# Landmarks laid over all 128 partitions, with the order of every engine's work written out

## The chip, the core and the metric

The kernel runs on one core of one Trainium2 chip. The metric is the device time of one execution in microseconds, lower is better, and the number that counts is the median over runs. In this text PE is the matrix engine (PEld its weight loads), ACT, DVE, POOL and SP are the other engines with their own instruction queues, and each of them takes its instructions strictly in the order in which the program has them.

## What is computed

Eight batches of attention through 32 landmark vectors per head, and then a two-layer network on the joined heads:

```python
def sm_attn(qq, kk, vv):
    s = scale * np.matmul(qq, kk.transpose(0, 1, 3, 2))
    a = softmax(s)
    return np.matmul(a, vv)
p_packed = sm_attn(p, k, v)              # p: (8, 8, 32, 64), q, k, v: (8, 8, 576, 64)
out = sm_attn(q, p_packed, p_packed)     # (8, 8, 576, 64)
x = out.transpose(0, 2, 1, 3).reshape(4608, 512)
h = x @ w_in                             # (512, 2048)
g = where(h >= 1, h, where(h <= -1, 0, (h + 1)**2 / 4))
result = g @ w_out                       # (2048, 512)
```

The landmarks are summed over in the second attention, so their order within a head can be any, as long as it is the same everywhere.

## The kernel before

**Tiles.** Everything is multiplied in bf16 with sums in f32. Tokens of a batch lie on 96 partitions. For each batch b (function `attention`, line 454) the keys and queries are transposed (tiles `tp`, `kT`, `qT`; on PE by line 471 for batches 0 and 1, by a transposing DMA of SP on line 500 for the others). Line 528 multiplies keys with landmarks into `sp` (four score tiles of a pair of heads each in batch 0), line 533 takes their exponentials `ex` on ACT, lines 619 and 624 form the packed values `pk`, line 634 the sums of the exponentials, and line 271 (a shared copy helper) casts them into `ppT`. Line 700 multiplies queries with `ppT` into `s`; on ACT follow the exponentials `eT` (line 723), the logarithm `ln` of their sums (line 732, sums `sm` on PE by line 728) and the reciprocal `rc` (line 737); DVE makes `A` from them (line 742). In place of out @ w_in, line 686 multiplies `ppT` with w_in into `mp`, which is cast to `M`: four chunks f of 512 hidden units. The function `hidden` (line 806) then does, for each of the 16 groups fi of 128 hidden units, four matmuls `h<-A,M` on PE (line 814), `x` on ACT (line 820), `t` on DVE (line 828) or on ACT (line 830), and `hT` on DVE (line 835). The function `output` (line 872) does 16 matmuls `o<-w_out_sb,hT` (line 889) for each tile of 128 tokens, a copy `ob` and a store (line 908). There are 36 such tiles, so 576 matmuls of 512 columns (608 instructions, since the last tile is done in three parts).

**Loads.** POOL issues the loads of k, q, v and of the weights (lines 352, 363, 368), which cast f32 to bf16 on the way. Eight of these may be under way; the ninth waits on POOL until the first has landed. The first half of batch 0's keys (`k_raw`) and the landmarks of batches 0 and 1 (`p_raw`) come as f32 over SP and ACT.

**Landmarks.** `p_raw` is a tile of 32 partitions (landmark), two batches, 8 heads by 64: two DMAs of 64 KB, one from SP and one from ACT (line 395). DVE casts it to `p_nat` (line 446); eight transposes of 32 rows on PE (line 426) put the head dimension on partitions (`tpp`), and four copies (line 271) place them into `pT`. The landmarks of batches 2 to 7 (`p_late`) come in six DMAs of POOL (line 375), four batches on 128 partitions and two on 64, with eight transposes (line 421) and four copies.

**What sets the order.** Each piece of work is a `Task` with a rank, the engines on which it can run and the time that each takes; a `Plan` runs through a model of the engines before anything is emitted, and at each step gives an engine that task of lowest rank among those that can start soonest (`run(slack)`). The program is then emitted in that order. The ranks are computed from the numbers `AT`, `HID`, `OUT` and `L1`. Where PE would wait before the first `o` matmul, the end of the kernel function fills the planned gap with matmuls on zeros (`o<-zeros`, line 942). PSUM has three wide buffers (tag `w`, for all of `tp`, `sp`, `pk`, `s`, `sm`, `mp`, `h` and a few `o`) and two narrow ones for `o`.

Of the kernel before, what the change touches and what calls it, by code (L numbers as in the profile page):

```python
# [11 lines left out]
class Task:  # L12
# [4 lines left out]
    def __init__(self, rank, ways, deps=(), takes=(), mode=None, behind=()):  # L17
        self.rank, self.ways, self.deps = rank, ways, list(deps)
        self.behind = [d for d in behind if d is not None]
        self.takes, self.frees, self.mode = list(takes), [], mode  # L20
        self.start = self.end = self.engine = None
        self.users = []


class Plan:
# [8 lines left out]
    CLAIM = 0.3  # L34
# [4 lines left out]
    def __init__(self, buffers):  # L39
# [8 lines left out]
    def add(self, rank, ways, deps=(), takes=(), mode=None, behind=()):  # L48
# [41 lines left out]
    def run(self, slack):  # L90
# [7 lines left out]
        ready = [t for t in self.tasks if not waiting[id(t)]]  # L98
        done = []

        def served(users):
            for u in users:
                waiting[id(u)] -= 1
                if waiting[id(u)] == 0:
                    ready.append(u)

        def finished(t):
# [5 lines left out]
            served(t.users)  # L113

        while len(done) < len(self.tasks):
            best = None
            found = defaultdict(list)
            left = {b: sorted(v) for b, v in self.slots.items()}
            for t in sorted(ready, key=lambda t: t.rank):
                at = max((d.end + self.LATENCY for d in t.deps), default=0.0)  # L120
                at = max([at] + [d.start + 0.001 for d in t.behind])
                need = defaultdict(int)
                for b in t.takes:
                    need[b] += 1
                short = any(len(left[b]) < n for b, n in need.items())
                wants = at < self.free["PE"] + self.CLAIM
                for b, n in need.items():
                    if not short:
                        at = max(at, left[b][n - 1] + self.LATENCY)
                    if wants:  # L130
                        del left[b][:n]
                if short:
                    continue
                for e in t.ways:
                    if e == "SP" and self.held is not None:
                        continue
                    start = max(self.free[e], at)
                    if e == "PE" and self.mode is not None and t.mode != self.mode:
# [839 lines left out]
```

## Time and profile before

| what | value |
|---|---|
| runs | 243.48, 244.42, 244.64 us; median 244.42 us |
| span of the profiled execution, first to last instruction | 241.1 us |
| between that span and the median | 3.3 us |
| PE busy / PEld busy | 97% / 56% of the span |
| ACT / DVE / POOL busy | 80% / 74% / 13% |
| granted PE clock | 1.00 |
| data moved by the DMA engines | 37.03 MB, mean 154 GB/s |

The page gives the profiled execution's span and no other time of it; the runs' times hold 3.3 us more than that span, which is work around the program that the profile doesn't show. A row of a timeline gives the start in us from the start of the span, the length, the engine, the line, the operation with its tiles, and in brackets how long the engine had been idle and what ended that. PE's busy time counts overlapping matmuls, so it says that PE had work in hand, not how fast it went; the distance between the starts of neighbouring matmuls tells that.

### The profile page before, as it was taken

To read this page: it belongs to the slowest core of one execution; us is meant where nothing else is said; L and a number is where in the kernel's file an instruction comes from. 1 tells how busy PE (TensorE), PEld (TensorE's weight loads), DVE (VectorE), ACT (ScalarE), POOL (GpSimd) and SP (SyncE) were. 2 spreads that over 40 slices of the span, in tenths; PEclk is the share of its full clock that TensorE was granted. 3 is DMA by queue.
4 is the path that set the end of the run, shared out by engine and by line. 5 is a ranking of instruction groups with operands and counts; after the bars stand their busy time and mean duration, and the time that the engine had idled before them with its cause. 6 is when DMAs were issued, how large, how long until landed. Compare 5 with 4: busy or idle time off the path is not lost.

```text
span 241.1 us, 5370 instructions
## 1 busy us (share of the span) xinstructions
PE 233.3 (97%) x2117; PEld 133.9 (56%) x2154; DVE 177.6 (74%) x311; ACT 192.7 (80%) x342; POOL 31.4 (13%) x47
## 2 busy tenths in 40 slices
PE   8999999999999999999999999999999999999995
PEld 2646555466554665466645564465546644565454
DVE  4549997678967998789936898689999955899000
ACT  3779996988969985999776988999789988888111
POOL 8462006200220040030030003000000000000000
PEclk9999999999999999999999999999999999999999
DMA  7999999996999999999999999999930301202233
GB/s 158 196 206 207 206 205 205 197 241 132 125 198 149 234 164 251 152 221 221 194 165 246 233 141 147 161 141 226 191 94 4 85 5 44 71 21 65 65 87 90
DMA packets 64138, 37.03 MB, mean 154 GB/s; under 512 B 36720, under 2 KB 59632, under 8 KB 64112
## 3 DMA queue, kind: packets, MB, share of 16 engines
q0 software_dynamic: 24336, 18.25, 52.6%
q1 hardware_dynamic: 38960, 17.87, 36.7%
q10 hardware_dynamic: 816, 0.56, 0.8%
q8 instruction: 17, 0.28, 0.5%
q14 instruction: 9, 0.07, 0.1%
HBM read 37.22 MB, written 9.44 MB: 194 GB/s over the span
## 4 chain that ended last, share of the span: by engine, by line
PE 81%; DVE 6%; DMA 5%; ACT 4%; POOL 2%; issue 2%; POOLq 0%; ACTq 0%
PE o L889 48%; PE h L814 21%; DMA w_in_sb<-in_moe_w_in_dram 5%; DVE hT L835 4%; PE mp L686 3%; PE pk L619 2%; PE sm L728 1%; DVE t L828 1%; ACT x L820 1%; PE sp L528 1%; PE s L700 1%; ACT t L830 1%; POOL q L352 1%; ACT M L271 1%; PE o L942 1%
## 5 line engine op out<-in xcount | busy, mean ns | idle before, releaser
L889 PE MATMUL o<-w_out_sb,hT 128*128 128x512 bf16 (+2 forms) x574 | 140.9, 367 | 1.9 <-issue 0.6
L835 DVE SCALAR_TENSOR_TENSOR hT<-t 128x576 bf16<-128x576 f32 (+1 forms) x130 | 93.7, 746 | 4.3 <-ACT t L830 2.3
L820 ACT ACTIVATE x<-h 128x576 f32<-128x576 f32 (+1 forms) x130 | 78.6, 651 | 9.1 <-PE h L814 8.5
L889 PEld LDWEIGHTS <-hT 128*128 128x128 bf16 x608 | 55.8, 98 | 49.8 <-issue 6.1
L814 PE MATMUL h<-A,M 128*128 128x288 bf16 x512 | 78.5, 286 | 0.6 <-ACT M L271 0.3
L814 PEld LDWEIGHTS <-M 128*128 128x128 bf16 x512 | 49.9, 98 | 27.6 <-issue 1.1
L830 ACT ACTIVATE t<-x 128x576 f32<-128x576 f32 (+1 forms) x57 | 39.4, 693 | 0.6
L828 DVE TENSOR_SCALAR t<-x 128x576 f32<-128x576 f32 (+1 forms) x73 | 33.3, 456 | 7.1 <-ACT x L820 6.7
L271 ACT COPY ob<-o 128x512 f32<-128x512 f32 (+2 forms) x22 | 12.0, 552 | 17.0 <-PE o L889 16.9
L742 DVE SCALAR_TENSOR_TENSOR A<-eT,rs,rc 128x576 bf16<-128x576 bf16 (+1 forms) x18 | 12.8, 748 | 11.5 <-ACT rc L737 11.5
L271 ACT CAST M<-mp 128x1024 bf16<-128x1024 f32 (+1 forms) x20 | 19.1, 992 | 2.7 <-PE mp L686 2.7
L352 POOL DMA_DIRECT2D k<-in_k_dram x8 | 6.7, 843 | 87.8 <-DMA kT<-k 68.4
L271 DVE CAST M<-mp 128x1024 bf16<-128x1024 f32 (+1 forms) x13 | 15.3, 1180 | 3.1 <-PE mp L686 3.1
L271 DVE COPY ob<-o 128x512 f32<-128x512 f32 x16 | 10.8, 688 | 6.9 <-PE o L889 6.9
L723 ACT ACTIVATE eT<-s,rs 128x576 bf16<-128x576 f32 x16 | 11.1, 742 | 2.5 <-PE s L700 2.5
L942 PE MATMUL o<-zeros 128*128 128x512 bf16 (+1 forms) x35 | 10.5, 431 | 1.3 <-DVE zeros L307 1.2
L732 ACT ACTIVATE ln<-sm 128x576 f32<-128x576 f32 x16 | 10.3, 652 | 1.2 <-PE sm L728 0.7
L686 PE MATMUL mp<-w_in_sb,ppT 64*32 64x512 bf16 x256 | 10.9, 380 | 0.2
L271 ACT CAST ppT<-pk 64x128 bf16<-64x128 f32 x24 | 6.2, 260 | 5.7 <-PE pk L634 4.0
L737 ACT ACTIVATE rc<-ln 128x576 f32<-128x576 f32 (+1 forms) x18 | 10.4, 625 | 0.1
L352 POOL DMA_DIRECT2D v<-in_v_dram x8 | 6.2, 779 | 21.9 <-PE pk L624 15.2
L533 ACT ACTIVATE ex<-sp 96x768 bf16<-96x768 f32 (+1 forms) x12 | 8.1, 709 | 0.5 <-PE sp L528 0.4
(59 smaller groups left out, 116.7 us busy)
## 6 DMA issues: line engine op xcount, KB each, us to landing
v<-in_v_dram POOLq DMA_DIRECT2D x8, 576.0 KB, 11.6
out_dram<-ob SPq DMA_DIRECT2D x23, 192.0 KB, 4.5
k<-in_k_dram POOLq DMA_DIRECT2D x7, 576.0 KB, 8.7
q<-in_q_dram POOLq DMA_DIRECT2D x7, 576.0 KB, 12.8
out_dram<-ob SPq DMA_DIRECT2D x24, 128.0 KB, 2.9
w_out_sb<-in_moe_w_out_dram POOLq DMA_DIRECT2D x4, 512.0 KB, 19.7
w_in_sb<-in_moe_w_in_dram POOLq DMA_DIRECT2D x3, 512.0 KB, 15.2
out_dram<-ob SPq DMA_DIRECT2D x23, 64.0 KB, 4.5
```

The costliest lines, as they stand in the source:

```text
L271: i = (nc.vector.tensor_copy if e == "DVE" else nc.scalar.copy)(to, of)
L352: G_.dma_start(tokens(nm, b)[:, heads(hs)], rows_of(nm, b, hs))
L686: m = nc.tensor.matmul(have["mp", b, f][a * NP:(a + 1) * NP, g], have["ppT", b][r, g, a], w_in_sb[r, a, f * FW:(f + 1) * FW], start=True, ...
L723: nc.scalar.activation(have["eT", b, g], have["s2", b, g][:, :, :HALF], AF.Exp, scale=rs_of[b][:, g, 1:])
L742: V.scalar_tensor_tensor(have["A", b][:, g, xs], have["eT", b, g][:, xs], rs_of[b][:, g, :1], have["rc", b, g][:, xs], ALU.mult, ALU.mult)
L814: nc.tensor.matmul(have["h", b, fi][:, hf, :HALF], have["M", b][:, g, fi * P:(fi + 1) * P], have["A", b][:, g, hf], start=(g == 0), stop=( ...
L820: nc.scalar.activation(have["x", b, fi][:, hs[0]:hs[-1] + 1], have["h", b, fi][:, hs[0]:hs[-1] + 1, :HALF], AF.Prelu, bias=-1.0, alpha=0.5)
L828: V.tensor_scalar(t, x, 1.0, 0.0, ALU.add, ALU.max)
L830: nc.scalar.activation(t, x, AF.Relu, bias=1.0)
L835: V.scalar_tensor_tensor(dst, t, 1.0, t, ALU.min, ALU.mult)
L889: nc.tensor.matmul(have["o", key][:, :w], hT[:, fi, i * P:(i + 1) * P], w_out_sb[:, fi, cols], start=(fi == 0), stop=(fi == KF - 1))
L942: nc.tensor.matmul(o[:, :w], zeros[:, :P], zeros[:, :w], start=True, stop=True)
```

## The change

Three things are changed together.

**Landmarks.** They now lie on 128 partitions as (head, pair of landmarks): partition h*16+m holds landmarks 2m and 2m+1 of head h, 128 numbers. Batches 0 and 1 come in one DMA from SP (nothing from ACT), batches 2 to 7 in one DMA from POOL. Each batch then takes one 128x128 transpose on PE: two at the start in place of eight, six later in place of eight. The copies into `pT` are eight at the start, four on DVE and four on ACT, each of half as many elements as before, and four later. The cast to `p_nat` has 256 elements per partition in place of 1024.

**Order.** `Task` takes its engine and its place from a table `ORDER` of numbers, one list for each group of tasks (a0 the attention of batch 0, h0 its hidden groups, o00 the first output tile). A number is the task's place on its engine; A or D behind it says ACT or DVE. `Plan.run` still goes through the model, for the fillers on zeros, and no longer chooses. A `t` or a cast can so change its engine: over the whole program 16 `t` go from ACT to DVE (57 to 41 on ACT, 73 to 89 on DVE), two casts of `M` from DVE to ACT, and one cast of `k` and one copy of `ob` of a full tile, and the three narrow copies of the last tile, from ACT to DVE.

**Loads.** Their order is part of the table.

The core of the diff; the table's two first attention lines stand for all of it:

```diff
     def __init__(self, rank, ways, deps=(), takes=(), mode=None, behind=()):
-        self.rank, self.ways, self.deps = rank, ways, list(deps)
+        self.rank, self.ways, self.deps = float(rank.rstrip("AD")), ways, list(deps)
...
+        self.engine = next(e for e in ways if len(ways) == 1 or e[0] == rank[-1])
...
-    AT = [dict(kT=148.161, qT=275.48, sc=149.063, pk=-49.085, s2=-3.905, sm=-182.602, M=178.569, **{"M+": -129.863}),
...
+    ORDER = """
+    first 0 0 0 1 5D 4D
+    load 1 2 0 3 4 6 5 7 9 8 10 11 12 13 14 15 16 20 21 19 17 22 18 24 23 25 26 27 28 29 30 31 32 33 34 35
+    p 1 0 1A 2D 3D 0A 132 75A 81D
+    a0 1 9D 6D 2 7D 8D 3 2A 11D 4 3A 10D 9 12D 8A 12 15D 10A 14 16D 12A 22 6 4 7 5 5 6 8 7 10 11 13D 9A 14 13 15 11 16
+        14 15 17 20 21 13 17 16 18 19 19 20 18 17A 19 18D 20 21A 38 35A 46 38A
...
-    p_raw = work.tile([NP, 2, H, D], f32, tag="vv", name="p_raw", bufs=BUFS["vv"])
-    p_nat = work.tile([NP, 2, H, D], bf16, tag="ln", name="p_nat", bufs=BUFS["ln"])
+    p_raw = work.tile([P, 2, X * D], f32, tag="vv", name="p_raw", bufs=BUFS["vv"])
+    p_nat = work.tile([P, 2, X * D], bf16, tag="ln", name="p_nat", bufs=BUFS["ln"])
+    p_rows = p.rearrange("b h (m j) d -> (h m) b (j d)", j=X)
...
-            have["p"] = work.tile([P, 2, H, D], bf16, tag="vv", name="p_late", bufs=BUFS["vv"])
-            for b in range(2, B):
-                i, r = divmod((b - 2) * NP, P)
-                G_.dma_start(have["p"][r:r + NP, i], p[b].rearrange("h n d -> n h d"))
+            have["p"] = work.tile([P, B - 2, X * D], bf16, tag="vv", name="p_late", bufs=BUFS["vv"])
+            G_.dma_start(have["p"], p_rows[:, 2:])
...
     def load_p_raw(e):
-        for i, queue in enumerate((nc.sync, nc.scalar)):
-            queue.dma_start(p_raw[:, i], p[i].rearrange("h n d -> n h d"))
+        nc.sync.dma_start(p_raw, p_rows[:, :2])
...
         def turn(e):
-            have["tpp", b0] = tp = wide([P, Q, 8 * NP] if b0 else [P, 8, Q, NP], bf16, "tpp")
...
-            for b in range(b0, b1):
-                for a in range(Q):
-                    nc.tensor.transpose(tp[:, b - b0, a],
-                                        p_nat[:, b, G * a:G * a + G].rearrange("n g d -> n (g d)"), ident[:NP, :NP])
+            have["tpp", b0] = tp = wide([P, b1 - b0, 1024 if b0 == 0 else P], bf16, "tpp")
+            for i in range(b1 - b0):
+                nc.tensor.transpose(tp[:, i, :P], of()[:, i], ident)
...
+        for bs in [range(b, b + 1) for b in range(b0, b1)] if b0 == 0 else [range(b0, b1)]:
+            out = []
+            for j in range(X):
+                c = len(bs) * H * NP // X
+                out.append(plan.add("p", either(
+                    (0.2 + c / 480, 0.2 + c / 480), (0.22 + c / 300, 0.3 + c / 300),
+                    *[(lambda x=x, j=j, bs=bs: pT[x * D:(x + 1) * D, bs[0]:bs[-1] + 1, :, :, x, j * NP // X:(j + 1) * NP // X],
+                       lambda j=j, bs=bs: have["tpp", b0][j * D:(j + 1) * D, bs[0] - b0:bs[-1] + 1 - b0, :P].rearrange(
+                           "p b (a g m) -> p b g a m", a=Q, g=G))
+                      for x in range(X)],
+                    parted=("tpp", b0)), [t, consts] + pads))
...
-    order = plan.run({"PE": 0.05, "ACT": 0.05, "DVE": 0.05, "SP": 0.0, "DMA": 0.0})
+    order = plan.run()
```

**POOL, the loads from the first one on.** The rows are POOL's queue before; 96x4x384 is four heads of batch 0, 96x8x384 a whole batch.

```order
L352 DMA k<-in_k_dram 96x4x384
L352 DMA v<-in_v_dram 96x8x384
L352 DMA q<-in_q_dram 96x4x384
L352 DMA q<-in_q_dram 96x2x384 x2
L363 DMA w_in_sb<-in_moe_w_in_dram 64x4x512 x2
L363 DMA w_in_sb<-in_moe_w_in_dram 128x4x512
L368 DMA w_out_sb<-in_moe_w_out_dram 128x4x512
L352 DMA k<-in_k_dram 96x8x384
```

The same place of POOL's queue in the changed kernel, whose lines have other numbers.

```order
L411 DMA q<-in_q_dram 96x4x384
L411 DMA k<-in_k_dram 96x4x384
L411 DMA v<-in_v_dram 96x8x384
L411 DMA q<-in_q_dram 96x2x384 x2
L422 DMA w_in_sb<-in_moe_w_in_dram 64x4x512 x2
L422 DMA w_in_sb<-in_moe_w_in_dram 128x4x512
L411 DMA k<-in_k_dram 96x8x384
L427 DMA w_out_sb<-in_moe_w_out_dram 128x4x512
```

Four heads of q have gone ahead of the keys and values of batch 0, and the keys of batch 1 ahead of the first chunk of w_out. Further on, batch 2 is loaded as k, q, p, v where it was v, q, p, k.

**ACT, from the scores of batch 0 to its first `x`.** ACT's queue before: the exponentials of the scores, the softmax of batch 0, the casts of `M` for f=0 (128x512) and f=1 (128x2x512).

```order
L533 ACTIVATE ex<-sp 96x12x32 x4
L271 CAST ppT<-pk 64x128 x2
L271 COPY qT<-tp 128x4x96
L271 COPY qT<-tp 128x288
L723 ACTIVATE eT<-s_321,rs 128x576
L732 ACTIVATE ln<-sm 128x576
L723 ACTIVATE eT<-s_347,rs 128x576
L737 ACTIVATE rc<-ln 128x288
L732 ACTIVATE ln<-sm 128x576
L271 CAST M<-mp 128x512
L737 ACTIVATE rc<-ln 128x288 x3
L820 ACTIVATE x<-h 128x288 x2
```

The same stretch of ACT in the changed kernel.

```order
L330 CAST ppT<-pk 64x128 x2
L330 COPY qT<-tp 128x288
L770 ACTIVATE eT<-s_320,rs 128x576
L330 COPY qT<-tp 128x288
L770 ACTIVATE eT<-s_349,rs 128x576
L779 ACTIVATE ln<-sm 128x576
L784 ACTIVATE rc<-ln 128x288
L779 ACTIVATE ln<-sm 128x576
L330 CAST M<-mp 128x512
L784 ACTIVATE rc<-ln 128x288 x3
L330 CAST M<-mp 128x2x512
L866 ACTIVATE x<-h 128x288 x4
```

The two `eT` now stand together ahead of the first `ln`, one more `qT` copy stands between them, and the cast of `M` for f=1 stands ahead of the first `x`. On PE the `mp` of f=1 stands ahead of the first `h` in the same way. In PE's queue up to the queries' transposes of batch 1 there are 33 `o` matmuls before and 31 in the changed kernel; the other work up to that point is the same in both, the landmarks' transposes and the fillers apart (34 of 512 columns and 4 of 256 before, 35 and 5 now).

More of the change, by code (lines that the diff above doesn't have):

```diff
@@ L150, in run @@
                 continue
-            assert best is not None, "no step can take its buffers"
+            assert best is not None, "the order of an engine waits for itself"
             at, t, e = best
-            if e == "PE" and t.mode != self.mode:
-                at = max(at, self.free[e] + self.SWITCH)
-            ready.remove(t)
+            lines[e].pop()
             keep, lasts = t.ways[e][:2]
-            t.start, t.engine, t.end = at, e, at + lasts
+            t.start, t.end = at, at + lasts
             self.free[e] = at + keep
@@ L411, with landmarks @@
     pT_of, pads = {}, []
[L413 to L414 removed]
+    def landmarks(b0, b1, of, deps):
         def turn(e):
[L417 to L444 removed]
```

337 lines of the change are left out of this document (188 added, 149 removed), and 7 rows, old and new, of the table OUT.

## The prediction

> **What bounds the kernel now.** I read the page first, then the busy times by stage, the waits of PE, the chain of work that ended last, and the timelines of the start and the end. The page and the table by stage (from, to, its length, then busy us of each engine):
>
> ```profile
> PE 233.3 (97%) x2117; PEld 133.9 (56%) x2154; DVE 177.6 (74%) x311; ACT 192.7 (80%) x342; POOL 31.4 (13%) x47
> ...
> L942 PE MATMUL o<-zeros 128*128 128x512 bf16 (+1 forms) x35 | 10.5, 431 | 1.3 <-DVE zeros L307 1.2
> ```
> ```profile
> 0.00:18.80 18.80, 16.84 (x200) 8.81 (x204) 8.98 (x31) 11.54 (x24) 11.94 (x21) 1.00 1.09 187
> 18.80:31.50 12.70, 11.99 (x126) 7.30 (x128) 11.96 (x24) 11.90 (x23) 1.67 (x2) 1.00 1.26 206
> 31.50:41.30 9.80, 9.67 (x123) 5.83 (x125) 8.45 (x14) 8.06 (x15) 3.29 (x6) 1.00 1.28 206
> 41.30:226.60 185.30, 183.28 (x1589) 105.06 (x1617) 148.25 (x245) 158.51 (x276) 14.52 (x19) 1.00 0.89 150
> 226.60:241.10 14.50, 11.47 (x84) 6.87 (x83) 0.00 (x0) 2.67 (x6) 0.00 (x0) 1.00 0.29 75
> ```
>
> PE's 97% holds 10.5 us of matmuls on zeros, nearly all in the first stage: up to 18.8 us little of its work is useful. Between 18.8 and 31.5 DVE and ACT are each busy 12 of 12.7 us, so there they set the pace, with the loads (DMA share over 1). From 31.5 us on only PE counts. Its waits from 31.6 us to the end, and two pieces of the chain that show its pace (start, length, what):
>
> ```profile
> PE o L889 <- issue: 0.6, 4, 0.2
> PE h L814 <- ACT M L271: 0.3, 1, 0.3
> ```
> ```profile
> 205.59 1.47 PE h L814 x12
> ...
> 219.47 7.12 PE o L889 x33
> ```
>
> All the named waits of 210 us come to 0.9 us; a matmul `o` takes 7.12/33 = 0.216 us and an `h` 1.47/12 = 0.123 us, 512 and 288 columns at the same 0.42 ns each. The end then is fixed work: what is left for PE at some moment after 31.5 us, plus the last copy and store.
>
> ```profile
> 238.15 0.27 ACT L271 COPY ob<-o 128x128 f32<-128x128 f32 x1 [0.58 <-PE o L889]
> 238.45 0.37 ACTq L908 DMA_DIRECT2D out_dram<-ob  x1
> ```
>
> So a change can gain only by getting the same PE work done earlier before about 41 us, or in the tail; it can lose anywhere. The start goes by these rows: POOL, PE and ACT in order of time, with what each had waited for.
>
> ```profile
> 1.48 0.81 POOL L352 DMA_DIRECT2D k<-in_k_dram  x1 [0.17 <-issue]
> ...
> 4.30 0.39 PE L426 MATMUL tpp<-ident,p_nat 32*128 32x32 bf16 x8
> ...
> 5.80 0.60 DVE L271 CAST k<-k_raw 96x768 bf16<-96x768 f32 x1 [0.50 <-DMA k_raw<-in_k_dram]
> ...
> 8.02 1.42 ACT L533 ACTIVATE ex<-sp 96x384 bf16<-96x384 f32 x3
> ...
> 9.85 0.49 ACT L533 ACTIVATE ex<-sp 96x384 bf16<-96x384 f32 x1 [0.41 <-PE sp L528]
> ...
> 10.42 0.84 PEld L624 LDWEIGHTS <-v 96*64 96x64 bf16 x48 [0.46 <-DMA v<-in_v_dram]
> ...
> 11.40 0.54 ACT L271 CAST ppT<-pk 64x128 bf16<-64x128 f32 x2 [1.06 <-PE pk L624]
> ...
> 12.45 0.82 ACT L271 COPY qT<-tp 128x384 bf16<-128x384 bf16 x2 [0.51 <-PE tp L471]
> ...
> 13.48 0.74 ACT L723 ACTIVATE eT<-s,rs 128x576 bf16<-128x576 f32 x1 [0.21 <-PE s L700]
> ```
> ```profile
> 16.50 0.65 ACT L732 ACTIVATE ln<-sm 128x576 f32<-128x576 f32 x1 [0.17 <-PE sm L728]
> ...
> 17.35 0.59 ACT L271 CAST M<-mp 128x512 bf16<-128x512 f32 x1 [0.20 <-PE mp L686]
> ...
> 17.84 1.11 ACT L737 ACTIVATE rc<-ln 128x288 f32<-128x288 f32 x3
> ...
> 18.87 0.65 PE L814 MATMUL h<-A,M 128*128 128x288 bf16 x4
> 19.31 0.71 ACT L820 ACTIVATE x<-h 128x288 f32<-128x288 f32 x2 [0.37 <-PE h L814]
> 19.45 0.11 PEld L686 LDWEIGHTS <-ppT 64*32 64x32 bf16 x8 [0.24 <-DMA w_in_sb<-in_moe_w_in_dram]
> ...
> 19.53 0.91 POOL L352 DMA_DIRECT2D q<-in_q_dram  x1 [1.62 <-DMA w_in_sb<-in_moe_w_in_dram]
> ...
> 19.93 1.01 ACT L271 CAST M<-mp 128x1024 bf16<-128x1024 f32 x1
> ...
> 29.82 0.11 PEld L686 LDWEIGHTS <-ppT 64*32 64x32 bf16 x8 [0.25 <-DMA w_in_sb<-in_moe_w_in_dram]
> ```
>
> The reader is to see who is waited for: values at 10.42, w_in f=1 at 19.45, f=3 at 29.82, each a landing. The landing times follow from the issues and the list of DMA issues up to 30 us (KB each, us to landing):
>
> ```profile
> q<-in_q_dram POOLq DMA_DIRECT2D x1, 576.0 KB, 21.1
> ...
> k<-in_k_dram POOLq DMA_DIRECT2D x1, 288.0 KB, 5.7
> q<-in_q_dram POOLq DMA_DIRECT2D x1, 288.0 KB, 8.6
> ```
>
> Keys of batch 0 land at 1.48 + 5.7 = 7.2 us, queries of batch 1 at 19.53 + 21.1 = 40.6 us.
>
> **The change, part by part.**
>
> *Landmarks at the start.* PE transposes them at 4.30 us, and the keys' cast waits for `k_raw` until 5.80 us. All that the shorter cast and the two transposes save comes before that wait, so nothing is gained; the eight copies of half the size are covered too, since the scores that read `pT` now stand behind keys that land at 8.5 us (below). Were that cover gone, four copies in a row at 0.4 us (an `rc` of 288 columns, the nearest row, is 1.11/3) would hold DVE's cast of the keys for 0.5 us. One side effect: ACT issues its half of `k_raw` first, and the landmarks come in fewer pieces, so POOL's stream of loads may run free a little sooner; I bound it by 0 and 0.5 us (DVE's wait for `k_raw`) and take 0.1 us, near the lower end, because q's landing below takes back part of it.
>
> The Trainium skill, "DMA: Bandwidth & Descriptors", section "Specifications", asks for pieces of at least 512 B for full rate; these grow from 256 to 512 B in DRAM, which would put the gain at its upper end and the sum 0.4 us lower. No row here times a landmark's DMA free of `k_raw`, so the trace neither bears this out nor speaks against it.
>
> *Landmarks of batches 2 to 7.* One issue in place of six on POOL, PE's eight transposes become six:
>
> ```profile
> 39.56 2.85 POOL L375 DMA_DIRECT2D p_late<-in_p_dram  x5
> ```
>
> Five of six issues cost POOL 2.85 us, and POOL is busy 3.3 of the 9.8 us there: off the path. Two transposes of 128 columns less are 2 x 128 x 0.42 ns = 0.1 us of PE, gained in the stage where PE counts.
>
> *Loads reordered.* Four heads of q (288 KB) now go ahead of k, and so do as k did: k lands later by what such a load takes in the stream. Before, q's four heads landed just behind the values: the third DMA, issued after two of 0.81 us at 3.1, landed at 11.7, and the values were waited for until 10.4, so 1.3 us. Keys then land at 8.5, values at 11.7; everything from w_in on keeps its bytes ahead of it, so f=1 and f=3 land as before, and so do the queries of batch 1.
>
> *Batch 0's scores.* In the table's line a0 the scores have PE's places 6, 7, 5, 8: those of heads 4 and 5 come first, and they need the late keys, while ACT takes the exponentials in order 0 to 3. Before, from landing (7.2) to the start of the last exponential (9.85) there were 2.65 us, with three exponentials (1.42 us) already done by 9.44. Now all four follow the late keys: 8.5, some 1.7 us for transposes, copies and first scores (2.65 less two exponentials of 0.47), and 4 x 0.48 us, which gives about 12.2 us for `pk`, against 10.42. The values at 11.7 are the lower bound, 12.7 the upper.
>
> *Up to the first `h`.* `pk` 12.2, its 48 matmuls (0.84 us) and casts (0.54): 13.7. The first `s`, which before stood behind q's copies (the 12.45 row), now waits for `ppT`; `eT` starts at about 14.2 in place of 13.48, half a microsecond after the casts, as `s` and the reciprocal lie between. The second `eT` stands behind four fillers on PE (4 x 0.216) and a `qT` copy: about 15.9 to 16.6. Then ACT's queue: `ln` 0.65, `rc` 0.4, `ln` 0.65, `M` 0.59, and two of the three `rc` (1.11/3 each): 19.6, and after DVE's `A` the first `h` at about 20.0 us, 1.1 later than 18.87. Moreover `M` of f=1 now precedes the first `x`: ACT is through with it at about 21.1 (before 20.94) with no `x` done, where before two (0.71 us) were. ACT is 0.9 us behind.
>
> *From 20 to 41 us.* Here the moved `t` pay back. The rows:
>
> ```profile
> L820 ACT ACTIVATE x<-h 128x576 f32<-128x576 f32 (+1 forms) x130 | 78.6, 651 | 9.1 <-PE h L814 8.5
> ...
> L830 ACT ACTIVATE t<-x 128x576 f32<-128x576 f32 (+1 forms) x57 | 39.4, 693 | 0.6
> L828 DVE TENSOR_SCALAR t<-x 128x576 f32<-128x576 f32 (+1 forms) x73 | 33.3, 456 | 7.1 <-ACT x L820 6.7
> ```
>
> Up to the cast of `M` for f=3 ACT had three and a half `t` (2.5 us) and now has one, but takes over the cast of f=2 (1.01 us): 0.8 us less. So it is some 0.1 to 0.4 us late there instead of 0.9. PE then does `mp` f=3 at about 30.2 (landing at 29.8 as before), and from there to `pk` of batch 1 it has 28 `h` (3.44 us) and 9 `o` (1.94 us), 0.43 us less than before with 11 `o`; before that stretch took 6.95 us with about 0.8 of stalls:
>
> ```profile
> 36.77 0.94 PE L624 MATMUL pk<-ex,v 96*64 96x32 bf16 x48
> ...
> 41.14 1.19 PE L471 MATMUL tp<-ident,q 96*128 96x96 bf16 x24
> ```
>
> That gives `pk` at 36.3, if nothing stalls between (36.1 to 37.4 with 0 and 1.1 us of stall). From `pk` to the transposes of q took 4.37 us and takes two `o` more, 4.80: they start at 41.1, as before, and can't start before q lands at 40.6. But by then 31 `o` are done where 33 were: 2 x 0.216 = 0.43 us are owed. This is the main term. Rounded: +0.4.
>
> *After 41 us.* PE's work is the same but for the transposes, and it had no waits to lose. ACT loses 16 x 0.69 = 11 us, DVE gains 16 x 0.46 = 7.3: both stay under PE. The order is new throughout; I take 0.1 us for new stalls, with 0 and 1 us as bounds. In the tail, DVE copies the last pieces; ACT took 0.27 us for one, and I take the same (bounds 0.1 either way).
>
> **Sum.** 0.4 - 0.1 (transposes) - 0.1 (stream) = +0.2; I take +0.3, since a small stall of the new order after 41 us is likelier than none: a span of 241.4 for 241.1, and with the 3.3 us around it 244.7 us for the median of 244.42.
>
> **Rivals.** Half a percent, 1.2 us, is what a measurement of this kernel can tell from no change.
>
> *The late start isn't absorbed (slower).* If the `x` and `hT` of batch 0 stay 1.1 us late until `pk` of batch 1, it starts at 37.4 and the transposes of q at 42.2: 1.1 + 0.4 owed, 245.9 us; a late `mp` or one more `o` without `hT` gives 246.2. It decides from `pk` of batch 1 later than 37.1. For it: DVE and ACT were busy 12 of 12.7 us there, DVE gets `t` as well as two clearings that it did in an idle moment before. Against: ACT is relieved, and w_in f=3 holds everything at 29.8 anyway. The Trainium skill, "TensorE: Matmul & The Clock Gate", section "Step-by-step: what each phase is for", says that matmuls stay in program order and only weight loads are pulled ahead. By that rule the `mp` of f=1, now ahead of the first `h`, holds it until 19.5 us whatever else is ready, which is inside this price. The trace agrees: at 19.45 PE waited 0.24 us for w_in.
>
> *PE has idle time that the new order removes (faster).* The stage 41.3 to 226.6 shows 185.30 - 183.28 = 2.02 us without PE busy. If these were waits and the order closed them all, 242.7 us. Against: the named waits are 0.9 us, and a gap of 0.2 us is as long as one `o` whose record is missing.
>
> *The change does nothing for time:* the landmarks are off the path, and the new start costs what the relieved ACT returns: 244.3, inside my forecast's range.
>
> **Numbers.** My forecast with the do-nothing case 0.70, the unabsorbed start 0.16, new stalls after 41 us of a microsecond or more 0.04, the closed gaps or a stream that starts earlier than I allow 0.10. The range leaves out most of the last case and the worst of the second: 243.5 to 246.2. Forecast alone: 243.9 to 245.3. Faster by over 0.5% 0.10, within 0.70, slower 0.20.
>
> **What would show it.** Keys of batch 0 landing at 8.5 and `pk` at 12.2; the first `h` near 20.0; `mp` f=3 near 30; `pk` of batch 1 near 36.3; q's transposes at 41.1; after that no waits of PE above 0.3 us. I am wrong if q's transposes come with 33 or more `o` done, or if PE waits after 41 us, or if it did before without my seeing it.

## The result, and the profile after

The changed kernel takes 258.5 us in the median of four runs (253.74 to 260.71), against 244.19 us for the kernel before beside it: a ratio of 1.0485, 95% interval 1.0394 to 1.0577. The forecast was 244.7 us, with 246.2 as its upper end: it was wrong by 14 us. The runs of the changed kernel lie up to 7 us apart, where those of the kernel before lie within 1.2; the ratio, here and below, is made only from runs within 1.5% of the shortest of their kernel, so versions are compared by their ratios and not by their medians. By the ratio the change costs 4.85%, some 12 us. The profiled execution took 257.43 us and its span is 255.7 us, 14.6 us longer than before.

Two things said above on the kernels are not right. In "k, q, p, v" for batch 2 the q is that of batch 3; the queries of batch 2 come behind v. And the 3.3 us between span and median are not all work around the program: here a run takes 1.7 us more than its own span, and nearly all later runs 1.7 to 2 us, so the profiled execution of the kernel before was probably some 1.5 us shorter than its median run.

The page, busy times and the clock by slices:

```profile
PE 240.3 (94%) x2148; PEld 135.8 (53%) x2148; DVE 180.7 (71%) x333; ACT 186.0 (73%) x324; POOL 28.8 (11%) x42
...
PEclk9999999999999799999999869999999999999999
```

There are two dips in the granted clock where before there was none. The same profile by stretches (from, to, its length, busy us of PE, PEld, DVE, ACT, POOL, then clock, DMA share, GB/s), cut where PE stood still:

```profile
31.50:41.20 9.70, 9.70 (x125) 5.77 (x123) 8.32 (x16) 7.87 (x15) 1.23 (x1) 1.00 1.29 206
41.20:81.60 40.40, 40.24 (x372) 23.34 (x371) 28.65 (x47) 33.93 (x55) 3.08 (x4) 1.00 1.32 176
81.60:86.30 4.70, 0.43 (x3) 0.13 (x2) 1.76 (x4) 0.74 (x2) 1.25 (x1) 1.00 1.05 194
...
141.30:145.70 4.40, 0.42 (x3) 0.14 (x2) 0.83 (x2) 0.50 (x2) 0.77 (x1) 0.86 0.71 169
```

Up to 41.2 us nothing is amiss. Then PE does 0.4 us of work in each of two stretches of over 4 us. Its two longest waits from 31.6 us on say for whom (total, times, longest):

```profile
PE h L860 <- ACT x L866: 4.3, 1, 4.3
PE o L939 <- DVE ob L330: 4.0, 1, 4.0
```

The start, on PE, against the forecast's places:

```profile
4.63 0.39 PE L473 MATMUL tpp<-ident,p_nat 128*128 128x128 bf16 x2 [1.12 <-DVE p_nat L494]
...
9.83 0.68 PE L519 MATMUL tp<-ident,k 96*128 96x96 bf16 x12 [0.52 <-DMA k<-in_k_dram]
...
13.42 0.94 PE L671 MATMUL pk<-ex,v 96*64 96x32 bf16 x48
...
20.56 0.66 PE L860 MATMUL h<-A,M 128*128 128x288 bf16 x4
...
30.40 0.41 PE L733 MATMUL mp<-w_in_sb,ppT 64*32 64x512 bf16 x8
...
36.40 0.94 PE L671 MATMUL pk<-ex,v 96*64 96x32 bf16 x48
...
41.19 1.19 PE L519 MATMUL tp<-ident,q 96*128 96x96 bf16 x24
```

The transposes of batch 1's queries start at 41.19 us (before 41.14) with 31 `o` done instead of 33: 0.5 us behind, as forecast. The loss comes later. The first wait, in the chain of work that ended last:

```profile
68.98 15.54 DMA v<-in_v_dram
84.54 0.56 DVE vv L649
85.56 0.66 ACT x L866
86.26 0.98 PE h L860 x4
```

The values of batch 3 are 15.5 us under way. DVE takes its work in order and stands at their copy `vv`; the `t` behind it are late, so ACT can't reuse its `x`, so PE gets no `h` emptied. The second wait, on DVE:

```profile
144.87 0.69 DVE L330 COPY ob<-o 128x512 f32<-128x512 f32 x1 [5.03 <-DMA out_dram<-ob]
```

The copy of a finished tile finds none of the four `ob` buffers free until a store has landed. What each wait leaves behind, in the 5 and 6 us after it, is a clock of 0.66 and 0.53:

```profile
86.30:91.30 5.00, 5.00 (x42) 3.16 (x42) 4.89 (x10) 3.49 (x7) 0.79 (x2) 0.66 1.06 159
...
145.70:151.70 6.00, 6.00 (x22) 2.95 (x22) 4.87 (x10) 2.39 (x4) 0.00 (x0) 0.53 1.09 171
```

That costs 5.0 x 0.34 + 6.0 x 0.47 = 4.5 us more. The Trainium skill, "TensorE: Matmul & The Clock Gate", section "What's actually happening", says that PE's clock is halved after an idle window of about 3.4 us and comes back after as long a busy one; both waits here are longer than that, and here the trace agrees with the rule. A shorter stop can do the same: in the run with the new order on the old landmarks, below, PE stands for 2.27 and for 2.17 us, and behind each the granted clock is 0.50 for 3.4 us (from 73.9 and from 176.3 us).

The account of the 14.6 us of span: 0.5 at the start, 4.3 + 4.0 in two waits, 4.5 of clock; of the 1.3 us that stay, 0.4 are a third wait for `ob`, some 0.3 come from a longer end (3.3 us behind PE's last matmul, 2.95 before), and the rest in gaps too small to name.

### The profile page after: what moved, and what is told of

It reads as the page before. It is cut to its first block, busy times and chain, and to the rows that moved or that the text cites. A ratio compares the mean times of both kernels' runs of the same rounds, so it can differ in the third digit from the quotient of the medians.

```text
span 255.7 us, 5395 instructions
## 1 busy us (share of the span) xinstructions
PE 240.3 (94%) x2148; PEld 135.8 (53%) x2148; DVE 180.7 (71%) x333; ACT 186.0 (73%) x324; POOL 28.8 (11%) x42
## 4 chain that ended last, share of the span: by engine, by line
PE 77%; DMA 13%; ACT 3%; DVE 3%; issue 1%; POOL 1%; SPq 0%; DVEq 0%; POOLq 0%; ACTq 0%
PE o L939 44%; PE h L860 22%; DMA v<-in_v_dram 6%; DMA out_dram<-ob 4%; DMA k<-in_k_dram 3%; PE mp L733 2%; DVE hT L881 2%; PE tp L519 2%; PE pk L666 1%; PE sm L775 1%; PE sp L576 1%; PE s L747 1%; ACT x L866 1%; PE o L990 1%; PE pk L671 1%
## 5 line engine op out<-in xcount | busy, mean ns | idle before, releaser
L939 PE MATMUL o<-w_out_sb,hT 128*128 128x512 bf16 (+2 forms) x608 | 148.8, 372 | 4.4 <-DVE ob L330 4.0
L860 PE MATMUL h<-A,M 128*128 128x288 bf16 x512 | 81.2, 292 | 4.5 <-ACT x L866 4.4
L874 DVE TENSOR_SCALAR t<-x 128x576 f32<-128x576 f32 (+1 forms) x89 | 38.7, 453 | 14.6 <-ACT x L866 14.0
L330 DVE COPY ob<-o 128x512 f32<-128x512 f32 (+2 forms) x20 | 12.6, 636 | 24.3 <-PE o L939 19.3
L876 ACT ACTIVATE t<-x 128x576 f32<-128x576 f32 x41 | 27.3, 682 | 0.8 <-DVE hT L881 0.5
L330 ACT COPY ob<-o 128x512 f32<-128x512 f32 x18 | 10.4, 586 | 15.5 <-PE o L939 14.3
L789 DVE SCALAR_TENSOR_TENSOR A<-eT,rs,rc 128x576 bf16<-128x576 bf16 (+1 forms) x18 | 12.8, 746 | 9.1 <-ACT rc L784 8.9
L330 DVE CAST M<-mp 128x1024 bf16<-128x1024 f32 (+1 forms) x11 | 12.9, 1170 | 2.1 <-PE mp L733 2.1
L990 PE MATMUL o<-zeros 128*128 128x512 bf16 (+1 forms) x40 | 12.7, 444 | 1.2 <-DVE zeros L367 1.2
L411 POOL DMA_DIRECT2D q<-in_q_dram x10 | 7.5, 754 | 38.1 <-DMA qT<-q 32.2
L649 DVE COPY vv<-v 96x1536 bf16<-96x1536 bf16 x12 | 6.6, 547 | 6.1 <-DMA v<-in_v_dram 6.1
## 6 DMA issues: line engine op xcount, KB each, us to landing
v<-in_v_dram POOLq DMA_DIRECT2D x8, 576.0 KB, 15.6
```

Source lines behind the costliest of these rows:

```text
L330: i = (nc.vector.tensor_copy if e == "DVE" else nc.scalar.copy)(to, of)
L411: G_.dma_start(tokens(nm, b)[:, heads(hs)], rows_of(nm, b, hs))
L789: V.scalar_tensor_tensor(have["A", b][:, g, xs], have["eT", b, g][:, xs], rs_of[b][:, g, :1], have["rc", b, g][:, xs], ALU.mult, ALU.mult)
L860: nc.tensor.matmul(have["h", b, fi][:, hf, :HALF], have["M", b][:, g, fi * P:(fi + 1) * P], have["A", b][:, g, hf], start=(g == 0), stop=( ...
L874: V.tensor_scalar(t, x, 1.0, 0.0, ALU.add, ALU.max)
L876: nc.scalar.activation(t, x, AF.Relu, bias=1.0)
```

## The experiments

The first theory: the new order, not the landmarks, costs the time, and it does so because the values of batch 3 and the stores land late. The rivals: the landmarks' layout costs, or the DMA engines are the bound.

### Landmarks alone, order alone

The changed landmarks with the places and the loads' order of before; the table's lines change throughout, like these two. (In the experiments' tables each place has its engine's letter, also where one engine alone can do the task; the letters by themselves change nothing.)

```diff
-    load 1 2 0 3 4 6 5 7 9 8 10 11 12 13 14 15 16 20 21 19 17 22 18 24 23 25 26 27 28 29 30 31 32 33 34 35
+    load 0 1 2 3 4 5 6 7 8 9 10 11 12 13 14 15 16 17 18 19 20 21 22 23 24 25 26 27 28 29 30 31 32 33 34 35
-    o00 33 36 40 49 54 60 73 74 75 76 81 84 86 96 97 103 65D 14
+    o00 32 37 38 41 65 66 77 78 79 82 83 84 96 97 98 99 59D 4
```

> The changed landmarks, but every engine's order and the loads' order as in the kernel before. Theory (the 14 us come from the new order alone: values of batch 3 and the stores of output tiles land late, and DVE, which works in order, then stands and stops PE twice): 243.7 to 245.0 us, ratio to before 0.997 to 1.003, no wait of PE above 1 us after 41 us. Rival (the landmarks' new layout costs): 246 us or more.

Measured: 244.29 us, ratio 1.003 (1.0011 to 1.0049). Its waits of PE from 31.6 us on:

```profile
PE h L860 <- ACT M L330: 0.3, 1, 0.3
```

The other half, the new order on the old landmarks:

```diff
-        nc.sync.dma_start(p_raw, p_rows[:, :2])
+        for i, queue in enumerate((nc.sync, nc.scalar)):
+            queue.dma_start(p_raw[:, i], p[i].rearrange("h n d -> n h d"))
...
+                for a in range(Q):
+                    nc.tensor.transpose(tp[:, b - b0, a],
+                                        p_nat[:, b, G * a:G * a + G].rearrange("n g d -> n (g d)"), ident[:NP, :NP])
```

> The new order of work and loads, but the landmarks as before (32 partitions, two transfers at the start, six later, eight transposes each). Theory: 254 to 260 us as in the changed kernel, with PE waiting about 4 us near 82 us and again near 141 us. Rival (the landmarks' layout costs): 250 us or less.

Measured: 254.97 us, ratio 1.0431 (1.0375 to 1.0486). The two largest waits of PE:

```profile
PE o L947 <- ACT ob L330: 4.4, 2, 2.3
PE pk L674 <- DMA ex<-exn: 1.9, 1, 1.9
```

The order holds nearly the whole loss, as the theory has it. But the waits are not where it has them: PE has none behind batch 3's values, and two for `ob` (the ACT copies) of at most 2.3 us. With 0.3% the landmarks cost a little too, where the forecast had them as a gain of 0 to 0.5 us.

### Take away the first wait

First by DVE's place for the copy of the values (place 103 of `a3` becomes 111.5):

```diff
-    a3 7 9 222 108 225 113 103 112 237 120A 117A 129 259 126 266 129 131 136 127 271 130 132 137 134D 277 133A 134A
+    a3 7 9 222 108A 225 113A 111.5D 112D 237 120A 117A 129D 259 126A 266 129A 131A 136D 127A 271 130A 132A 137D 134D
```

> The changed kernel, but the first copy of batch 3's values into vv stands later in DVE's queue, behind five t and three hT more, so that DVE does not stand still for values that land at 84.5 us. Theory: the wait of PE near 82 us (4.3 us) goes and with it some 1 to 2 us of half clock behind it: 250.5 to 253 us. The second wait near 141 us stays. Rival (the DMA engines are the bound and the waits only show where it surfaces): the time moves to another wait, 256 to 258 us.

Measured: 256.55 us (253.04 to 258.6), so the forecast's 250.5 to 253 us was missed. Waits of PE:

```profile
PE o L939 <- DVE ob L330: 4.2, 1, 4.2
PE o L939 <- ACT ob L330: 2.2, 1, 2.2
```

Then by the loads:

```diff
-    load 1 2 0 3 4 6 5 7 9 8 10 11 12 13 14 15 16 20 21 19 17 22 18 24 23 25 26 27 28 29 30 31 32 33 34 35
+    load 1 2 0 3 4 6 5 7 9 8 10 11 12 13 14 15 16 20 21 19 17 22 18 23 24 25 26 27 28 29 30 31 32 33 34 35
```

> The changed kernel, but the values of batch 3 are loaded ahead of the queries of batch 4, as before the change; nothing else differs. Theory: the values land some 5 us sooner (79 to 80 us instead of 84.5), the wait of PE near 82 us shrinks from 4.3 to under 1 us: 250.5 to 254 us. Rival (the transposing DMA beside the load holds it, whichever load it is): the values still land after 83 us, 256 to 259 us.

Measured: 257.15 us, ratio 1.059 (1.0538 to 1.0641); the forecast was 250.5 to 254 us. DVE's copy of the values, and PE's waits:

```profile
79.73 0.81 DVE L649 COPY vv<-v 96x1536 bf16<-96x1536 bf16 x1 [1.21 <-DMA v<-in_v_dram]
```
```profile
PE o L939 <- DVE ob L330: 5.3, 1, 5.3
PE o L939 <- ACT ob L330: 2.6, 1, 2.6
```

Both edits do what they should: PE's wait behind the values' copy is gone, and with the second the values come at 79.7 us. Yet nothing is won that these runs can show, since PE now waits for `ob`. So the values' lateness is not a loss of its own; this part of the theory fell. Left are the two that share SP's queue and the DMA engines: the stores out of the `ob` buffers, or the traffic itself.

### The stores

SP's queue shows why the buffers are full. SP before, and SP of the changed kernel (start, length, what; two stores are one tile in two pieces):

```profile
45.12 11.05 SPq L908 DMA_DIRECT2D out_dram<-ob  x8
56.29 3.14 SPq L500 DMA_TRANSPOSE kT<-k  x1
```
```profile
49.73 0.81 SPq L957 DMA_DIRECT2D out_dram<-ob  x2
50.67 5.98 SPq L548 DMA_TRANSPOSE kT<-k  x1
...
84.68 7.57 SPq L957 DMA_DIRECT2D out_dram<-ob  x4
92.35 7.75 SPq L548 DMA_TRANSPOSE kT<-k  x1
100.19 5.44 SPq L957 DMA_DIRECT2D out_dram<-ob  x8
```

Before, the stores of four tiles went ahead of the first transpose; now one tile's does. And the order of the stores is another matter. The last number of an `o` line in the table is SP's place, the one ahead of it the copy's place:

```
    o00 33 36 40 49 54 60 73 74 75 76 81 84 86 96 97 103 65D 14
    o05 195 197 200 201 215 218 219 221 223 226 228 229 230 231 232 233 118D 13
    o16 329 332 333 335 336 340 341 344 345 346 354 355 356 358 359 361 167A 35
    o20 434 436 437 439 440 442 443 445 446 448 450 452 453 454 455 456 204A 34
```

The tile o00 is the second that PE finishes and is copied before 50 us:

```profile
48.41 1.29 DVE L330 COPY ob<-o 128x512 f32<-128x512 f32 x2 [0.23 <-PE o L939]
```

But its store has place 14, behind that of o05, the ninth tile: it is among the eight stores issued from 100.19 us on, so a buffer is held for some 50 us by a finished tile. In the same way o16 waits behind o20 and o22 behind o27. In the kernel before SP issues stores in the order in which PE finishes the tiles. Two theories follow: (A) the stores' order holds the buffers, (B) the transposes ahead of the stores do; (C) is the DMA bound.

SP's column put in PE's order, same places for the transposes:

```diff
-    o00 33 36 40 49 54 60 73 74 75 76 81 84 86 96 97 103 65D 14
+    o00 33 36 40 49 54 60 73 74 75 76 81 84 86 96 97 103 65D 5
-    o16 329 332 333 335 336 340 341 344 345 346 354 355 356 358 359 361 167A 35
+    o16 329 332 333 335 336 340 341 344 345 346 354 355 356 358 359 361 167A 26
```

> The changed kernel with one column of its table altered: SP issues the stores of the output tiles in the order in which PE finishes the tiles (o03 o00 o02 o01 ...), in the same 38 places of SP's queue; the transposes keep their places. In the changed kernel the store of o00 stands behind that of o05, o16 behind o20, o22 behind o27, so that a finished copy in one of the four ob buffers waits about 50 us for its store. Theory A (stores out of order hold the ob buffers): no wait of PE for ob above 1 us near 90, 141 or 171 us; the wait for batch 3's values near 82 us may stay; 246 to 252 us. Theory B (the transposes ahead of the stores on SP hold them): the ob waits stay, 254 to 259 us. Theory C (the DMA engines are the bound): 254 us or more, with the wait at some other place.

Measured: 250.24 us, ratio 1.0254 (1.0216 to 1.0291). Waits of PE, in a profiled run that was the longest of the four (253.77 us):

```profile
PE o L939 <- DVE ob L330: 3.2, 1, 3.2
PE o L939 <- ACT ob L330: 1.7, 1, 1.7
```

The time is what A forecast, and under the 254 us that B and C gave as their least: by the ratios 2.3%, some 5.6 us, less than the changed kernel. But 2.5%, some 6 us, over the kernel before stay, and in that run PE waits for `ob`, which A had at no more than 1 us; so B may have a part as well. With the values' copy later besides:

```diff
-    a3 7 9 222 108A 225 113A 103D 112D 237 120A 117A 129D 259 126A 266 129A 131A 136D 127A 271 130A 132A 137D 134D 277
+    a3 7 9 222 108A 225 113A 111.5D 112D 237 120A 117A 129D 259 126A 266 129A 131A 136D 127A 271 130A 132A 137D 134D
```

> The stores in order as in the run before, and also the first copy of batch 3's values later in DVE's queue. Theory A: both waits gone, no wait of PE above 1.5 us after 41 us: 243.5 to 247 us. Theory B: 251 us or more, with ob waits. Theory C: the time moves to another wait, 250 us or more.

Measured: 254.46 us, ratio 1.0357 (1.0288 to 1.0427): not faster than the run before, from which the interval does not set it apart, and far from A's 243.5 to 247 us. In its profiled run (255.25 us) PE still waits 3.5 us and 1.7 us for `ob`. A alone does not suffice; what came is B's forecast (251 us or more, with waits for `ob`), and this run by itself does not exclude C's 250 us or more. More buffers instead of another order:

```diff
-    BUFS = dict(w=3, o=2, k=1, q=2, v=1, vv=1, kT=2, qT=2, ex=2, ks=2, ppT=2, M=2, A=2, eT=4, ln=2, rc=2, x=4, t=4, ob=4)
+    BUFS = dict(w=3, o=2, k=1, q=2, v=1, vv=1, kT=2, qT=2, ex=2, ks=2, ppT=2, M=2, A=2, eT=4, ln=2, rc=2, x=4, t=4, ob=7)
```

> The changed kernel with seven ob buffers for four; order untouched. Theory A: three more buffers are as many as the late stores hold at a time (one or two), so the ob waits go and the wait for batch 3's values near 82 us stays alone: 247 to 252 us. Theory B: seven buffers also cover a store that leaves 15 to 26 us late: the same, 247 to 252 us; this run does not tell A from B. Theory C (DMA bound): buffers only move the wait: 254 us or more.

Measured: 252.87 us median, from 249.94 to 258.02, between the two forecasts. The largest wait of PE in the profiled run (250.10 us):

```profile
PE pk L666 <- DMA ex<-exn: 3.7, 1, 3.7
```

No wait for `ob` is left: the buffers were short because of the late stores. But another DMA of SP's queue, the transpose `ex`, is now late. And the reverse, in the order of before: two stores moved back, nothing else.

```diff
-    o00 32 37 38 41 65 66 77 78 79 82 83 84 96 97 98 99 59D 4
+    o00 32 37 38 41 65 66 77 78 79 82 83 84 96 97 98 99 59D 14.2
-    o16 340 341 342 343 344 345 346 347 348 349 350 351 352 353 354 355 167A 23
+    o16 340 341 342 343 344 345 346 347 348 349 350 351 352 353 354 355 167A 32.2
```

> The reverse: the changed landmarks with the order of before (244.3 us), but two stores moved back on SP as the changed table has them: that of o00 behind o05, that of o16 behind o20. Theory A: an ob buffer is held from 47 to about 90 us and from 122 to about 152 us, three buffers are left, PE waits for ob copies at one or two places for 2 to 5 us each: 247 to 254 us. Theory B or C (only the transposes or the loads matter): 243.7 to 245 us.

Measured: 252.17 us, ratio 1.0329 (1.0291 to 1.0368). The wait on ACT, that on PE, and SP's queue around it:

```profile
84.96 0.58 ACT L330 COPY ob<-o 128x512 f32<-128x512 f32 x1 [5.21 <-DMA out_dram<-ob]
```
```profile
PE h L860 <- ACT x L866: 4.9, 1, 4.9
```
```profile
78.95 1.40 SPq L957 DMA_DIRECT2D out_dram<-ob  x2
...
84.92 12.98 SPq L957 DMA_DIRECT2D out_dram<-ob  x10
```

Two stores in the wrong place of SP's queue cost 3%, some 7 us, in an order that loses 0.3% with the stores in place. This shows A by itself. It also teaches how such a wait is read: PE names ACT's `x`, and the cause is several steps back. A copy stands ahead of `x` on ACT; it finds no buffer until the store issued from 78.95 us on has landed; and it needs that store's buffer because one of the four is still held by o00, copied at 48 us, whose store is the last of the ten pieces issued from 84.92 us on.

### Stores by readiness, and the landmarks' transfer

Now B: stores in PE's order and each ahead of the transposes that become ready after its copy (kT and qT of batch 4 go from places 12 and 17 to 15 and 18, for instance).

```diff
-    o00 33 36 40 49 54 60 73 74 75 76 81 84 86 96 97 103 65D 14
+    o00 33 36 40 49 54 60 73 74 75 76 81 84 86 96 97 103 65D 3
-    o16 329 332 333 335 336 340 341 344 345 346 354 355 356 358 359 361 167A 35
+    o16 329 332 333 335 336 340 341 344 345 346 354 355 356 358 359 361 167A 24
```

> The changed kernel with SP's column of the table rewritten: stores in the order in which PE finishes the tiles, and each store ahead of those transposes that become ready later than its copy (two to three tiles further ahead than in the run with stores in order alone). PE, DVE, ACT and the loads keep the changed order. If the stores' places on SP are the whole of the loss after 41 us: no wait of PE for ob above 0.5 us, 244 to 246.5 us. If the order on the compute engines or the loads cost as well: waits for other things, 248 us or more.

Measured: 248.03 us (244.48 to 248.44), ratio 1.0184 (1.0154 to 1.0214). The wait for `ob` went, as the first forecast has it; the time is that of the second. Waits of PE from 31.6 us on:

```profile
PE h L860 <- ACT x L866: 1.0, 1, 1.0
PE s L604 <- DMA kT<-k: 0.6, 1, 0.6
```

No wait for `ob` is left and the clock is 1.00 over the whole span. PE, ACT, DVE and the loads keep the changed order, so the 3% between the ratios 1.0485 and 1.0184, some 7 us, were the places of stores and transposes on SP, with the clock behind them; 0.7% of it came with the step from stores in order to stores by readiness, which speaks for a part of B. C, the DMA engines as the bound, gave 254 us or more to the stores in order; both runs lie under that. Of the 3.9 us by which the span of the profiled run (245.0 us) exceeds that of the kernel before, PE's named waits after 31.6 us are 1.6. With seven `ob` buffers on top:

```diff
-    BUFS = dict(w=3, o=2, k=1, q=2, v=1, vv=1, kT=2, qT=2, ex=2, ks=2, ppT=2, M=2, A=2, eT=4, ln=2, rc=2, x=4, t=4, ob=4)
+    BUFS = dict(w=3, o=2, k=1, q=2, v=1, vv=1, kT=2, qT=2, ex=2, ks=2, ppT=2, M=2, A=2, eT=4, ln=2, rc=2, x=4, t=4, ob=7)
```

> Stores by readiness as above, with seven ob buffers. If ob buffers still limit with the stores by readiness: faster than that run by 1 us or more. If not: within 1 us of it.

Measured: 247.86 us, ratio 1.0148 (1.0106 to 1.019): within 1 us, and the intervals overlap, so no limit by the buffers shows any more.

The landmarks' 0.3% was tried in the order of before, with the first landmarks in two transfers:

```diff
-        nc.sync.dma_start(p_raw, p_rows[:, :2])
+        for i, queue in enumerate((nc.sync, nc.scalar)):
+            queue.dma_start(p_raw[:, i], p_rows[:, i])
```

> The changed landmarks with the order of before (244.3 us, 0.3% over before), but the first landmarks in two transfers of 64 KB, from SP and from ACT, as before the change. There p_raw landed at 4.3 us where it had at 3.1, PE waited 1.2 us more for p_nat and ran its fillers at half pace behind that. If the single transfer is the cause of the 0.3%: p_raw lands by 3.4 us, the first h comes below 19.3 us, 243.3 to 243.9 us. If the copies or transposes in the new layout are the cause: 244.1 to 244.6 us.

Measured: 244.0 us, ratio 1.0017 (0.999 to 1.0043). PE with one transfer, and then with two:

```profile
4.70 0.39 PE L473 MATMUL tpp<-ident,p_nat 128*128 128x128 bf16 x2 [1.19 <-DVE p_nat L494]
4.89 3.19 PE L990 MATMUL o<-zeros 128*128 128x512 bf16 x7
7.88 1.51 PE L519 MATMUL tp<-ident,k 96*128 96x96 bf16 x18
...
20.08 0.74 PE L860 MATMUL h<-A,M 128*128 128x288 bf16 x4
```
```profile
3.51 0.39 PE L474 MATMUL tpp<-ident,p_nat 128*128 128x128 bf16 x2
...
19.31 0.65 PE L861 MATMUL h<-A,M 128*128 128x288 bf16 x4
```

The trace shows the mechanism: PE waits 1.2 us, the seven fillers behind that take 3.19 / 7 = 0.46 us each (an `o` of the same size takes 0.216), and the keys' transposes come at 7.9 us. Two transfers bring the first `h` from 20.08 to 19.31 us (18.87 before). In time the run lies between its two forecasts and the two intervals overlap, so the gain isn't shown. Both together, stores by readiness and two transfers:

```diff
-        nc.sync.dma_start(p_raw, p_rows[:, :2])
+        for i, queue in enumerate((nc.sync, nc.scalar)):
+            queue.dma_start(p_raw[:, i], p_rows[:, i])
...
-    o00 33 36 40 49 54 60 73 74 75 76 81 84 86 96 97 103 65D 14
+    o00 33 36 40 49 54 60 73 74 75 76 81 84 86 96 97 103 65D 3
```

> Stores by readiness, and the first landmarks in two transfers from SP and ACT. If both costs add: 0.5 to 1.2 us less than with stores by readiness alone, 243 to 245.5 us. If the late queries and keys of batch 0 hold the start anyway: no difference from that run.

Measured: 246.48 us, ratio 1.0115 (1.0086 to 1.0143), by the ratios 1.7 us under the run without; the two intervals do not overlap. So the second transfer is worth something in this order, but the time is 1 us over the forecast's upper end. The last 1.15%, some 2.8 us, were sought with two more edits on top of that version, the second with both:

```diff
-    a3 10 12 222 108A 225 113A 103D 112D 237 120A 117A 129D 259 126A 266 129A 131A 136D 127A 271 130A 132A 137D 134D
+    a3 10 12 222 108A 225 113A 111.5D 112D 237 120A 117A 129D 259 126A 266 129A 131A 136D 127A 271 130A 132A 137D 134D
```

> Stores by readiness, the first landmarks in two transfers (246.5 us together), and the first copy of batch 3's values later in DVE's queue. In the run before PE still waited 1.2 us near 82 us for an x that stood behind this copy. If that wait is a loss of its own: 244.8 to 245.8 us, no wait there. If the values' lateness only shows at the next reader: 246 to 247 us.

Measured: 246.1 us (243.79 to 261.62), ratio 1.0086 (1.0054 to 1.0118). In the profiled run, one of 255.37 us, the wait for `x` is gone, and PE stands for a transpose of SP's queue instead:

```profile
PE pk L667 <- DMA ex<-exn: 6.9, 1, 6.9
```

Then the order of the loads as well:

```diff
-    load 1 2 0 3 4 6 5 7 9 8 10 11 12 13 14 15 16 20 21 19 17 22 18 24 23 25 26 27 28 29 30 31 32 33 34 35
+    load 0 1 2 3 4 6 5 7 9 8 10 11 12 13 14 15 16 20 21 19 17 22 18 23 24 25 26 27 28 29 30 31 32 33 34 35
```

> All of that, and the loads nearer to the order of before: the four heads of batch 0's queries behind its keys and values, the values of batch 3 ahead of the queries of batch 4. If what is left over the kernel before lies in the order of the loads (late keys at the start, late values near 80 us): 243.4 to 244.6 us. If it lies in the order on PE, ACT and DVE: within 0.5 us of the run beside it.

Measured: 245.89 us (244.19 to 249.79), ratio 1.0076 (1.0041 to 1.0111). Neither run is set apart from the one before it: the intervals overlap, and single runs lie 5 to 18 us apart. So about 2 us over the kernel before stay open. The trace of the version ahead of these two edits names a part: its last matmul ends at 240.47 us, 2.3 us later than before (238.13), with 0.4 us owed at the queries' transposes (41.07 us, 31 `o` done) and 1.2 us in one wait for `x`. The rest may lie in the order on the compute engines, which wasn't taken apart. No version here beats the kernel before.

## Why the prediction was wrong

**Right: where the kernel stands at 41 us.** `pk` of batch 1 at 36.40 us (forecast 36.3), the queries' transposes at 41.19 (41.1), with 31 `o` done: the main term, +0.4, stands. On the way the keys were waited for until 9.8 us (8.5 forecast), `pk` came at 13.42 (12.2) and the first `h` at 20.56 (20.0). The delay at the start was larger than forecast and was absorbed all the same, for the reason given against the first rival: w_in f=3 holds everything (POOL's next load waited for its landing until 30.04 us, and its `mp` came at 30.40, 30.2 forecast). That the last step agrees to 0.1 us is in part luck: by the rows given, the stretch from there to `pk` is 6.95 - 0.8 - 0.43 = 5.7 us without a stall, which gives 35.9 and not the 36.1 or 36.3 of the text; it took 6.0.

**The step that failed:** "I take 0.1 us for new stalls, with 0 and 1 us as bounds", and the reason given for it, that PE "had no waits to lose". The two long stalls and their clock came to 12.8 us in the profile. What the runs show in its place: 3% of the 4.85% go when only the places on SP are put right, and 3% come when two stores are moved back in the order of before. That a kernel has no waits tells that its order of transfers fits its buffers, not that there is room. The bound of 1 us had no row behind it. There are four `ob` buffers, and a store that leaves SP several tiles late takes one of them away, whatever PE's own order is. The table's SP column, which tells this, is used in the forecast for none of the 38 stores; only POOL, ACT and PE are compared in their order. New stalls of a microsecond or more had a chance of 0.04. The test named in the forecast, "if PE waits after 41 us", is the one that showed it wrong.

**Wrong in a small term: the landmarks.** Bounded by a gain of 0 to 0.5 us and taken as -0.1 (and another -0.1 for the transposes), they cost 0.3% (0.1 to 0.5%). The step saw that the copies and transposes were covered until `k_raw`, but not that one transfer in place of two lands later: `p_nat` came 1.1 us later, and PE's `tpp` stood waiting for it. Whether that is the one transfer itself or ACT's half of `k_raw`, now issued beside it at 0.77 us (behind `p_raw` at 1.23 before), no run separates. The rule of the Trainium skill on pieces of 512 B ("DMA: Bandwidth & Descriptors", "Specifications") can now be weighed: with pieces of 512 B on the same two queues the cast of `p_nat` starts at 3.16 us,

```profile
3.16 0.29 DVE L495 CAST p_nat<-p_raw 128x256 bf16<-128x256 f32 x1 [0.77 <-DMA p_raw<-in_p_dram]
```

against 3.21 with pieces of 256 B. In the three other traces with pieces of 512 B on two queues it starts between 3.02 and 3.14 us, in the one other with 256 B at 3.28: a gain of the sign that the rule gives, but of 0.05 to 0.26 us and not of 0.5.

**The rivals.** The unabsorbed start did not come: `pk` of batch 1 came at 36.40, well ahead of the 37.1 from which it decides. Nor did the closed gaps. The end, with DVE's copies of the last pieces, was bounded by 0.1 us either way: DVE's copy takes 0.29 us for ACT's 0.27, and the 0.3 us more behind PE's last matmul are mostly the landing of the last store.

## What to carry to other kernels

Where an order is written out, compare every queue that holds a buffer, the one that issues stores above all: walk through it and ask of each store how many tiles are copied between its own copy and its issue, and whether the ring has as many buffers. A wait in a profile is a symptom of the place where the queue breaks first; taking it away helps only if the queue behind it is not full as well, which two experiments here showed by moving the wait instead of removing it. In the traces here the granted clock was halved at every stop of PE of 2.3 us or more behind the start, for 3.4 us or two or three times that, and at none under 2 us; the two stops of about 4 us in the changed kernel (4.3 and 4.0 us, and 4.5 us of clock) were so paid about one and a half times.

## What was not expected of the hardware

A transposing DMA holds SP's queue for very different times. Two rows of SP in the changed kernel, of the same size:

```profile
57.56 2.97 SPq L548 DMA_TRANSPOSE qT<-q  x1
...
73.26 11.32 SPq L548 DMA_TRANSPOSE qT<-q  x1
```

While SP was at the first, no load moved data; the second ran beside the load of batch 3's values, which took 15.5 us (median of the eight loads of values: 11.6 before, 15.6 here). A load beside it isn't all: the transpose of keys at 68.43 us had one beside it too and took 3.41 us. In the stretch of the second the DMA engines were as busy as ever and moved half of what they do in a good stretch (share and GB/s, last two columns; first the changed kernel, then the one before):

```profile
73.20:84.70 11.50, 8.79 (x75) 5.01 (x74) 3.87 (x6) 6.89 (x11) 0.00 (x0) 1.00 1.36 115
```
```profile
80.00:84.00 4.00, 3.95 (x36) 2.63 (x36) 3.96 (x9) 4.00 (x8) 0.00 (x0) 1.00 1.24 246
```

Why it is so slow in one place and not in another wasn't tried; no run here set a transpose alone against one beside a load, with all else the same.
